# A fused forward and backward block on one core: a modulation row's ring moved behind the last fold, a fold through its other work tile, and bias rows in four row tiles

## The chip, the core and the metric

The kernel runs on one core of a Trainium2 chip. The metric is device time in microseconds of one execution. A core has a matrix engine (PE, with its weight loads PEld), a vector engine (DVE), a scalar engine (ACT), a general engine (POOL) and a sync engine (SP). Each executes its own instructions strictly in its own order; SP and POOL also issue the DMA transfers, so a transfer that waits on such a queue holds up all that stand behind it.

## The reference

One adaLN-conditioned block, forward and backward, batch 1, 2048 tokens, width 1024, hidden width 3584, all inputs in bf16:

```
mod = silu(c) @ w_mod                    # six rows of 1024: sa, ca, ga, sb, cb, gb
h = layernorm(x)*(1+ca) + sa
x = x + ga * irfft2(rfft2(h) * (w_r + 1j*w_i))
h = layernorm(x)*(1+cb) + sb
x = x + gb * (gelu(layernorm(h) @ w1 + b1) @ w2 + b2)
```

The outputs are x and the gradients, for a given grad_out, of x, w_r, w_i, w1, b1, w2, b2, c and w_mod. The gradient of w_mod is, for each of the six rows, an outer product of silu(c) with the gradient of that row, and the gradient of c needs the product of w_mod with it.

## The kernel before

The tokens are treated in four blocks of 512 (`NB = 4`), the hidden width in 28 chunks of 128, in groups of four (seven groups). A tile framework orders each engine's instructions from the order of the Python code and from priorities; `ordered()` (L670) pins PE's order by hand. It adds the waits: an instruction waits for the last writer of what it reads and for the last reader of what it overwrites. Tiles with the same `tag` share memory: a new one waits until the old one is no longer used.

The stages that matter here, in the order of time:

- **Forward MLP, about 388 to 768 us.** A written plan interleaves `z_block` (L782, the first product and the gelu) with `bo_pass` (L829, the second product). A `bo_pass` handles one block and one half (512 columns) of the width: four PSUM tiles `pbs`, one for each 128 tokens. Each is opened by a product of a row of ones with the bias row `b2_row` (L834, contraction length 1), and then accumulates 28 products (L843). ACT empties `pbs` (L852). At the end of a pass, `pa` (L862) sums over tokens, in four column tiles of 32. There are eight passes, so 32 bias products.
- **Backward through w1, block 0, about 768 to 820 us.** `pg_pass` (L934) multiplies the stored hidden gradient `gzr` (loaded from `d_gz`, L917) by w1, in two halves. ACT empties the result into `gn3` with row sums (L948). In the midst of it, `gmod5` (L994) reduces the gradient of modulation row 5 from `gacc`, stores it to `d_gmod` (L179), and runs `gmod_ring` (L968) for this row.
- **`gmod_ring`.** It loads the row into all partitions (`gr`, L976), and for each of eight 128-row parts of w_mod: loads the part (L973) into one of three buffers, reduces it against the row on DVE (L984), overwrites the buffer with the row times silu(c) (L986), and stores it to the output (L987, POOL). A buffer is loaded anew when its store has landed. In `gmod5` the buffers are `gmw` and `gmg`, in tags "ph" and "sb".
- **Backward blocks, about 820 to 1054 us** (the loop at L1080). For each block: loads of `n3u`, `n2u`, `got` (the output gradient), `pg_pass` for blocks 1 to 3; then on DVE and ACT the layer-norm gradient `ln_bwd` (L1026: a reduction L1028, two small steps L1030 and L1031, ACT L1032, and L1033); column sums over tokens on PE in strips of 32 columns (`sums3`, L196, into `acc3a`; `sums3_ga` into `acc3b`); a second layer-norm gradient (L1121); the add of the residual; the store of the sum to `d_gx1` (L1125, POOL); and then the fold: `g2` times the row `ga`, `fold_tok`, and `fold_d` into `fbuf2[:, b]`. All elementwise operations of two tensors go through `tt` (L172), so the profile shows them as L173. The fold works on two tiles, `g2` and `ftmp`; in block 3 `ftmp` is the tile of `gzr0`, which then becomes `ws2`.
- **Backward spectral part, from about 1054 us.** `s_fwd` (L466) multiplies `fbuf2` with a cosine or sine matrix (`pu`, L471, two PSUM tiles), emptied into `U` (L642); then eight `pair` steps with loads of `ws2` (L489 on SP, L490 on POOL), `pf` (L492) and so on. Between its steps PE is filled with products for the gradients of w2 (`gw2_product`, L1074) and w1. Each w2 chunk `fc` is emptied by ACT into `gwo[fc % 2]` (L1070) and stored by POOL (L1072). Their inputs come by transposing loads on SP (`hht`, `hhsA`, `otl` from `d_hh`, L1203; the first two into `fbuf2`, L1048). `gmod_ring` for rows 3 and 4 (`rows34`) runs beside the pairs, with buffers `gmy` and `sacc` in the tile `otl`, which has the memory of `got`.

## Time and profile before

| | us |
|---|---|
| three runs | 1496.75 (median), 1495.99, 1502.4 |
| the profiled execution | 1498.73 |
| its span, first to last instruction | 1496.9 |
| PE busy | 1407.9 (94%), 6703 instructions |
| DVE busy | 1069.7 (71%) |
| ACT busy | 721.7 (48%) |
| POOL busy | 359.1 (24%) |
| DMA | 324.27 MB, mean 217 GB/s |
| mean granted PE clock | 0.978 |

A "wait" is idle time of an engine ahead of an instruction, with what ended it. Products are pipelined: one of 128x512 is shown with 0.38 us, and at full clock they start 0.216 us apart.

### The profile page before, as it was taken

To read this page: it belongs to the slowest core of one execution; us is meant where nothing else is said; L and a number is where in the kernel's file an instruction comes from. 1 tells how busy PE (TensorE), PEld (TensorE's weight loads), DVE (VectorE), ACT (ScalarE), POOL (GpSimd) and SP (SyncE) were. 2 spreads that over 40 slices of the span, in tenths; PEclk is the share of its full clock that TensorE was granted. 3 is DMA by queue.
4 is the path that set the end of the run, shared out by engine and by line. 5 is a ranking of instruction groups with operands and counts; after the bars stand their busy time and mean duration, and the time that the engine had idled before them with its cause. 6 is when DMAs were issued, how large, how long until landed. Compare 5 with 4: busy or idle time off the path is not lost. (4 is left out here: it accounts for less than half of the span.)

```text
span 1496.9 us, 18191 instructions
## 1 busy us (share of the span) xinstructions
PE 1407.9 (94%) x6703; PEld 655.5 (44%) x6835; DVE 1069.7 (71%) x1574; ACT 721.7 (48%) x960; POOL 359.1 (24%) x421
## 2 busy tenths in 40 slices
PE   5899989999899999999999599999999999899998
PEld 2434545444344444444344244444444444444443
DVE  5883777898799888877411888987177676898533
ACT  4765546757787756666202133333622444453211
POOL 5710541211113122212111010021134421222323
PEclk8999999999999999999999799999999999999999
DMA  9962563899776777786997464396389977775995
GB/s 337 280 213 62 156 219 127 268 241 345 233 249 213 242 241 237 236 270 199 278 278 224 162 239 155 127 267 155 99 195 243 250 228 216 172 195 159 271 207 180
DMA packets 358040, 324.27 MB, mean 217 GB/s; under 512 B 209063, under 2 KB 300733, under 8 KB 357696
## 3 DMA queue, kind: packets, MB, share of 16 engines
q1 hardware_dynamic: 324160, 207.71, 51.8%
q0 software_dynamic: 33792, 115.40, 22.2%
q8 instruction: 53, 0.87, 0.2%
q14 instruction: 35, 0.29, 0.1%
HBM read 162.05 MB, written 111.20 MB: 183 GB/s over the span
## 5 line engine op out<-in xcount | busy, mean ns | idle before, releaser
L679 PE MATMUL pp<-gBoT,wt 128*128 128x512 bf16 x878 | 197.0, 381 | 5.1 <-DMA wt<-in_B_w_dram 2.1
L940 PE MATMUL pg<-w1T,gzr 128*128 128x512 bf16 x876 | 199.1, 386 | 1.3 <-issue 0.4
L1241 PE MATMUL gw1acc<-gzh,n3n 128*128 128x512 bf16 x876 | 194.5, 380 | 1.2 <-issue 0.2
L940 PEld LDWEIGHTS <-gzr 128*128 128x128 bf16 x896 | 88.0, 99 | 111.1 <-issue 10.8
L796 PEld LDWEIGHTS <-w 128*128 128x128 bf16 x896 | 87.7, 98 | 110.6 <-issue 7.2
L679 PEld LDWEIGHTS <-wt 128*128 128x128 bf16 x896 | 87.8, 98 | 109.3 <-issue 4.8
L1241 PEld LDWEIGHTS <-n3n 128*128 128x128 bf16 x896 | 87.7, 98 | 105.4 <-issue 1.8
L796 PE MATMUL pz<-n3Ta,w 128*128 128x512 bf16 x437 | 99.4, 383 | 4.4 <-ACT gt L799 3.5
L796 PE MATMUL pz<-n3Tb,w 128*128 128x512 bf16 x439 | 98.4, 379 | 0.5
L1065 PE MATMUL gw2acc<-gB,hhsA 128*128 128x512 bf16 x438 | 97.6, 379 | 0.7 <-issue 0.2
L843 PEld LDWEIGHTS <-hhA 128*128 128x128 bf16 x608 | 59.4, 99 | 74.4 <-issue 5.1
L799 ACT ACTIVATE gt<-pz,b_col 128x512 bf16<-128x512 f32 x112 | 73.1, 684 | 34.5 <-PE pz L796 31.4
L805 ACT ACTIVATE gt<-gt 128x2048 bf16<-128x2048 bf16 x28 | 53.5, 1910 | 67.0 <-DVE gt L173 67.0
L1245 ACT CAST gwo<-gw1acc 128x512 bf16<-128x512 f32 x53 | 30.7, 583 | 112.6 <-PE gw1acc L1241 87.4
L173 DVE TENSOR_TENSOR gt<-gt,gt 128x2048 bf16<-128x2048 bf16 x56 | 68.5, 1223 | 21.6 <-ACT gt L807 20.9
L173 DVE TENSOR_TENSOR ct<-ct 128x2048 bf16<-128x2048 bf16 x64 | 75.9, 1220 | 9.6 <-ACT ct L632 8.4
L1070 ACT CAST gwo<-gw2acc 128x512 bf16<-128x512 f32 x54 | 29.9, 584 | 99.6 <-PE gw2acc L1065 48.4
L1065 PEld LDWEIGHTS <-hhsA 128*128 128x128 bf16 x448 | 43.7, 98 | 52.1 <-DMA hhsA<-d_hh 0.6
L801 ACT ACTIVATE gt<-gt 128x2048 bf16<-128x2048 bf16 x28 | 53.4, 1908 | 0.6
L807 ACT ACTIVATE gt<-gt 128x2048 bf16<-128x2048 bf16 x28 | 53.4, 1907 | 0.5
L1246 POOL DMA_DIRECT2D out_dram<-gwo x56 | 30.7, 550 | 78.4 <-ACT gwo L1245 49.6
L1065 PE MATMUL gw2acc<-gB,otl 128*128 128x512 bf16 x187 | 44.0, 390 | 3.5 <-DMA otl<-d_hh 2.0
(318 smaller groups left out, 2496.0 us busy)
## 6 DMA issues: line engine op xcount, KB each, us to landing
gzr<-d_gz SPq DMA_DIRECT2D x28, 512.0 KB
wblk<-in_w_mod_dram SPq DMA_DIRECT2D x12, 1024.0 KB
d_ph<-pho POOLq DMA_DIRECT2D x21, 512.0 KB
out_dram<-otl POOLq DMA_DIRECT2D x40, 256.0 KB
d_hh<-hhA POOLq DMA_DIRECT2D x19, 512.0 KB
w2sD<-in_B_w_dram SPq DMA_DIRECT2D x14, 512.0 KB
hhC<-d_ph SPq DMA_DIRECT2D x14, 512.0 KB
w2sA<-d_ph SPq DMA_DIRECT2D x14, 512.0 KB
```

The lines of the kernel that those rows point to most:

```text
L173: return nc.vector.tensor_tensor(out=out, in0=a, in1=b, op=op)
L679: last_pe[0] = nc.tensor.matmul(pp[:], lhsT=wt[:, fg % 2, cch, k * P:(k + 1) * P], rhs=gBoT[j][:, cch, :], start=(cch == 0), stop=(cch == ...
L796: last_pe[0] = nc.tensor.matmul(pz[:], lhsT=w1s[g][:, cch, k * P:(k + 1) * P], rhs=n3T[:, cch, :], start=(cch == 0), stop=(cch == NDC - 1))
L799: nc.scalar.activation(out=zb[:, k, :], in_=pz[:], func=ACT.Identity, bias=b1_col[:, fc:fc + 1], scale=1.0)
L801: nc.scalar.activation(out=av, in_=zb, func=ACT.Square)
L805: nc.scalar.activation(out=sg, in_=bv, func=ACT.Sigmoid, scale=2.0 * GK)
L807: nc.scalar.activation(out=bv, in_=bv, func=ACT.Sigmoid, scale=-2.0 * GK)
L843: last_pe[0] = nc.tensor.matmul(pbs[i][:], lhsT=hh[:, k, i * P:(i + 1) * P], rhs=wp[:, k, :], start=False, stop=(g == 6 and k == 3))
L940: last_pg[0] = nc.tensor.matmul(pgs[i][:], lhsT=gzs[b, g][:, k, i * P:(i + 1) * P], rhs=w1Ts[g][:, k, h * KH:(h + 1) * KH], start=(g == 0 ...
L1065: nc.tensor.matmul(acc[:], lhsT=hh_of(fc)[:, t, :], rhs=gBs[t // 4][:, t % 4, h * KH:(h + 1) * KH], start=(t == 0), stop=(t == NT - 1))
L1241: nc.tensor.matmul(acc[:], lhsT=n3ns[t // 4][:, t % 4, cch * P:(cch + 1) * P], rhs=gz2[t // 8][:, t % 8, :], start=(t == 0), stop=(t == NT ...
L1245: nc.any.tensor_copy(out=ob, in_=acc[:])
```

## The change

Three edits:

1. The four token groups of a `bo_pass` get their bias from four copies of `b2_row`, in partitions 0, 32, 64 and 96, and each of the four products is placed in its own part of 32 rows of the array (`tile_position=(32 * i, 0)`). The row is loaded four times.
2. In the backward blocks, the first product of the fold (`g2` times `ga`) is written into `ftmp` instead of back into `g2`, and `fold_tok` and `fold_d` get the two tiles with their roles swapped.
3. `gmod_ring` for row 5 no longer runs in `gmod5`, but right ahead of where `rows34` is made, after the loop over the backward blocks, and with the buffers `gmy` and `sacc`. The reduction of the row and its store to `d_gmod` stay where they were.

```
-    b2_row = small.tile([1, D], BF16, name="b2_row", tag="gmrow", bufs=1)
+    b2_row = small.tile([P, D], BF16, name="b2_row", tag="gmrow", bufs=1)
     def after_ph():
-        nc.sync.dma_start(out=b2_row[:], in_=B_b2.rearrange("(o n) -> o n", o=1))
+        for i in range(4):
+            nc.sync.dma_start(out=b2_row[32 * i:32 * i + 1, :], in_=B_b2.rearrange("(o n) -> o n", o=1))
...
         for i in range(4):
             with ordered():
-                last_pe[0] = nc.tensor.matmul(pbs[i][:], lhsT=ones_bf[0:1, :], rhs=b2_row[0:1, cs_], start=True, stop=False)
+                last_pe[0] = nc.tensor.matmul(pbs[i][:], lhsT=ones_bf[32 * i:32 * i + 1, :],
+                                              rhs=b2_row[32 * i:32 * i + 1, cs_], start=True, stop=False,
+                                              tile_position=(32 * i, 0))
...
         store_gmod(g5, 5)
-        gmw = reg.tile([P, 2, D], BF16, name="gmw", tag="ph")
-        gmg = reg.tile([P, 2, D], BF16, name="gmg", tag="sb")
-        for _ in gmod_ring((5,), [gmw[:, 0], gmw[:, 1], gmg[:, 0]], gmg[:, 1, :]):
-            pass
...
         tt(au[:], g2[:], au[:], ALU.mult)
-        tt(g2[:], g2[:], bcn(ga_row, 4), ALU.mult)
-        fold_tok(g2, ftmp)
-        fold2_in[b] = fold_d(fbuf2[:, b], g2[:], ftmp)
+        tt(ftmp, g2[:], bcn(ga_row, 4), ALU.mult)
+        fold_tok(ftmp, g2[:])
+        fold2_in[b] = fold_d(fbuf2[:, b], ftmp, g2[:])
...
+    for _ in gmod_ring((5,), gmy, sacc):
+        pass
     rows34 = gmod_ring((3, 4), gmy, sacc)
```

In the built program the orders of PE and of ACT are the same as before, instruction for instruction. On DVE the ring's first reduction now stands after `fold_tok`'s first two steps of the last block, its first scaling after the next two, its second reduction after `fold_d`'s first two, and the other six steps behind the last fold; also the product into `gB3` stands two steps later in block 2's fold. On SP the ten loads of the ring left the stretch behind L1084 and L1086; the first transposing load into `fbuf2` comes ahead of `got`'s, the `gzr` loads of block 1 follow each other, and the first `pf` load is early, where a load of `gmg` was. The ring's loads now stand behind the four stores of `d_gmod` rows (L207): the row, one transposing load of `hht`, three w_mod loads, then one among the loads of `ws2`, and four ahead of those of `smi` and `hhsA`. On POOL the order behind the last store to `d_gx1` was three stores of `gwo` (chunks 3, 4, 5), four `ws2` loads, two stores of `gwo` (6, 7); it is now two stores of `gwo`, the ring's first store, four `ws2` loads, a store of `gwo`, three of the ring, one of `gwo`, three of the ring, one of `gwo`, one of the ring.

## The prediction

> **What bounds the kernel now.** I read the busy row first: PE works 1407.9 of 1496.9 us, so nearly every us that PE waits is a us of the span. PE's waits of over 0.3 us are 73 us together. The chain of waits (start, length, what) shows the largest of them:

> ```profile
> 801.76 7.33 SPq L1048
> 809.19 3.96 DMA gmg<-d_gmod
> 813.27 1.23 DVE gmw L984
> ```

> A transpose on SP's queue, then the load of the modulation row, then the ring of row 5 on DVE. PE's timeline (start, length, instructions, in brackets the idle time before) shows what hangs on it:

> ```profile
> 819.56 3.84 PE L940 MATMUL pg<-w1T,gzr 128*128 128x512 bf16 x17
> 839.97 0.61 PE L196 MATMUL acc3a<-gn3a,ones_bf 128*32 128x512 bf16 x2 [16.57 <-DVE gn3a L1033]
> ...
> 894.46 0.39 PE L196 MATMUL acc3a<-gn3b,ones_bf 128*32 128x512 bf16 x2 [2.65 <-DVE gn3b L1033]
> ...
> 948.70 0.39 PE L196 MATMUL acc3a<-gn3a,ones_bf 128*32 128x512 bf16 x2 [1.98 <-DVE gn3a L1033]
> ```

> In each backward block PE's first strip sum waits for DVE's first layer-norm gradient (L1033): 16.57, 2.65 and 1.98 us. DVE's timeline says why:

> ```profile
> 784.87 0.68 DVE L178 CAST row<-pq 1x512 bf16<-1x512 f32 x1 [0.18 <-PE pq L999]
> 813.27 1.23 DVE L984 CUSTOM_DVE_ANT_0 gmw<-gmw,gmg 128x1024 bf16<-128x1024 bf16 x1 [27.72 <-DMA gmg<-d_gmod]
> ...
> 834.15 1.22 DVE L1028 CUSTOM_DVE_ANT_0 got<-gn3a,n3u 128x1024 bf16<-128x1024 bf16 x1
> ...
> 877.02 2.29 DVE L173 TENSOR_TENSOR gn3a<-gn3a,rows 128x4096 bf16<-128x4096 bf16 x1 [3.02 <-DMA d_gx<-gn3a]
> ```

> DVE stands 27.72 us at the head of the ring, runs it to 834.15, and only then starts block 0, though ACT had emptied the products by 820.2. The last row is the fold's first product, in place, waiting for the store of the same tile. A wait also costs clock (window, length, busy times and counts, granted clock, DMA):

> ```profile
> 840.00:844.00 4.00, 3.78 (x10) 1.36 (x11) 3.77 (x8) 0.43 (x1) 0.00 (x0) 0.50 0.50 178
> 844.00:848.00 4.00, 4.00 (x20) 1.82 (x19) 3.13 (x3) 1.94 (x2) 0.00 (x0) 1.00 0.12 41
> ```

> After the 16.57 us, products run at half the granted clock, 0.43 us apart, then at full clock 0.216 us apart. The same happens after 2.65 us (0.53 at 895 to 898) and 1.98 us (0.50 at 950 to 953).

> **Row 5's ring leaves block 0.** PE and ACT have the same instructions in the same order in both programs. DVE loses at this place eight pairs of 1.22 + 0.48 us and all waits on them. The layer-norm gradient then needs the last evacuation, 820.2; from the first L1030 to the strip sum took 837.06 to 839.97, 2.9 us; so the strip can start near 823.6, and PE is there at 819.56 + 3.84 = 823.4. The wait falls from 16.57 to 0.2: **-16.4**. From this strip to the next ones PE took 839.97 to 851.17, 11.2 us, for 42 products; at full clock 42 x 0.216 + 0.6 = 9.7: **-1.5**. The next strips need pru, 9.7 us after the first strip (849.65): just in time. Loads: SP's queue loses ten ring loads, some of which waited for stores. The first hh transpose moves ahead of got's load into a gap where SP waited (782.4 to 796.5); the gzr loads of block 1 no longer stand between ring loads and come when PE frees the slots, to 819. The bounds are 0 (something else as late as the ring) and 18.1 us.

> **The fold's first product into the other tile.** It no longer waits for the store; the next step does, since it writes the stored tile. Of the 3.02 us (2.78 in block 1) the 2.29 us of the product are hidden. DVE ends each block 2.3 us earlier and PE, without the slow clock, 1.5 us earlier. In block 1 DVE's two L1028 (2.4 us) and the small steps then still end after PE's evacuation, so a wait of about 1.0 of 2.65 stays; in block 2 about 0.3 of 1.98. Waits of 0.82 and 1.27 us later in the trace (1182, 1216) are followed by full clock, so the slow 1.5 us go too: **-3.1 and -3.2**. Bounds: 0, if DVE stays as far behind, and -7.6, both waits and both slow stretches gone. In block 3 PE waits for nothing here.

> [...]

> **The ring behind the last fold.** Two of its reductions and one scaling now stand inside the last fold on DVE: 2 x 1.22 + 0.48 = 2.9 us, against 2.3 hidden there. From the end of the residual add (1032.8) to fbuf2 complete (1054.1) it was 21.3 us; now 21.9. By then PE is 24.2 us earlier than before and DVE 26.0 (22.7 at the start of block 2, 1.0 in its waits for PE's strips and evacuations, 2.3 in its fold), so pu isn't late by that. The ring's first loads go out when got is free (the same 1032.8), the w_mod ones behind one hht transpose (3.6 to 6 us on SP, rows 1032.84 and 1036.54); they land some 10 us after, and the reduction stands at 11.8 because the 1 MB store took 9.1. So they are just covered; each us later is a us on fbuf2, beyond 1 us of slack. What follows on SP (smi, two hhsA) has some 14 us of slack before PE needs it. The rest of the ring, six steps, lies where DVE was idle for 15.3 and 15.7 us (1054 to 1085).

> The new wait is on POOL. ACT and POOL, before:

> ```profile
> 1044.45 0.54 POOL L1072 DMA_DIRECT2D out_dram<-gwo  x1 [9.38 <-ACT gwo L1070]
> 1054.35 1.02 POOL L490 DMA_INDIRECT ws<-in_A_w_r_dram,xu  x1 [9.36 <-DVE fbuf L173]
> ...
> 1050.90 0.59 ACT L1070 CAST gwo<-gw2acc 128x512 bf16<-128x512 f32 x1 [2.86 <-PE gw2acc L1065]
> 1054.37 0.59 ACT L1070 CAST gwo<-gw2acc 128x512 bf16<-128x512 f32 x1 [2.88 <-PE gw2acc L1065]
> 1055.18 0.59 ACT L642 CAST U<-pu 128x512 bf16<-128x512 f32 x1 [0.22 <-PE pu L471]
> ```

> The store of gw2's chunk 5 (1044.45) left ahead of the four ws loads. In the new order it stands behind the ring's first store and those four. Counted from the residual add: scaling done at 15.9, gzr0 free and ws loads from 18.3, four times 1.3, the store at 23.5, landed at 26 to 28. ACT's two gwo casts of chunk 7 write the same slot and wait for it, and the U casts stand right behind them, due at 24.0. pu has two buffers, so PE waits about 3.5 us at its third column block, plus 1.5 of slow clock: **+5.0**, between 0 (store of gx1 lands in 6 us, as in other blocks) and +10.

> **b2's rows in four tiles.** Three more 2 KB loads near 111 us, where SP then idles to 126: nothing. On PE (first two rows the bias, last two a column-tiled sum):

> ```profile
> 743.03 1.03 PE L834 MATMUL pbo<-b_row,ones_bf 1*128 1x512 bf16 x4
> 743.99 3.63 PE L843 MATMUL pbo<-w2sC,hhA 128*128 128x512 bf16 x16
> ...
> 751.00 0.40 PE L862 MATMUL pa<-otile,ones_bf 128*32 128x512 bf16 x4
> 751.33 3.63 PE L843 MATMUL pbo<-w2sB,hhB 128*128 128x512 bf16 x16
> ```

> The bias occupies 0.96 us, the four column tiles 0.33. Row tiles don't occur in the trace; four products in four parts of the array are nearest to the latter, so 0.63 per group. Of eight groups six count (460, 520, 567, 620, 667, 743 us), since 388 is ahead of a wait for ACT (3.54 us at 407) and 713 holds one (1.86 us): **-3.8**. Bounds: -5.0, all eight; +2.3, if each of the four positions costs the 0.095 us that entering and leaving cost now, and nothing overlaps.

> [...] The trace shows 0.31 instead of 0.216 us on both sides of the present group already, so nothing is added.

> **Sum.** -16.4 - 1.5 - 3.1 - 3.2 + 5.0 - 3.8 = -23.0 us on the profiled execution of 1498.73: 1475.7. The median of the runs is 2.0 us lower: **1474**.

> **Rivals.**
> - The tiles don't overlap: PE's -3.8 falls away, 1478. For it: no row tile in the trace. Against: the column tiles.
> - POOL's order costs nothing: without +5.0, 1469. For it: other gx1 stores landed in 5.8 to 7.0 us, which brings all of that chain forward by 2 to 3 us. Against: the 9.1 us came with hht transposes on the same DMA engines, and these stay.
> - DVE is the bound of blocks 1 and 2, and the fold's 2.3 us go to something else that is late (au, a gzr tile): without -6.3, 1480. For it: DVE is busy 8 to 9 tenths of these slices. Against: the store is its longest wait in each fold, and the other inputs landed before they were needed.
> - Slower: the ring's loads come late at the last fold. DVE runs in order, so fbuf2, the ws loads, the chunk 5 store and PE's pu all wait. With X us of lateness the time is 1474 + X - 1: slower than before from X = 24, by over 0.5% from 31. For it: DVE stood 27.72 us for such a row, and 24.1 us for another in the tail (gr). Against: that was SP's order; from its issue the row landed in 4 us. With X = 33, 1506.

> **Chances.** Forecast 0.54 (own range 1470 to 1478, with tile and store bounds), tiles 0.10, no POOL wait 0.12, DVE-bound 0.16, ring late 0.08. About 0.5% (7.5 us) is what a measurement of this kernel can tell from no change. The first four lie below 1489; I move 0.04 of the DVE case, whose lateness may be larger, to no change, with 0.03 of the ring's: faster 0.88, same 0.07, slower 0.05. The range, 1466 to 1486, takes in the ends of the bias tiles and of the POOL wait and the DVE case.

> **What would show it.** The first strip sum near 820 us (3.8 earlier by the tiles) with under 0.5 us before it; granted clock 1.00 from there; the next two with 1 us or less; no DMA row ahead of the fold's first product, a short one ahead of its second step; at pu an idle of 3 to 4 us with ACT waiting for out_dram<-gwo; L834's four starting within 0.02 us. Wrong would be a new wait of several us in block 0 or 1, or DVE idle for otl inside the last fold.

## The result, and the profile after

The changed kernel takes 1483.89 us (median of 6 runs, 1479.81 to 1487.43) against 1497.95 us of the kernel before in the same comparison: ratio 0.9906, 95% interval 0.9879 to 0.9934, so 14 us faster, where the forecast had 23. 1483.89 lies inside the forecast's range of 1466 to 1486 us, but not inside 1470 to 1478, the range of the main case alone. The profiled execution is the slowest of the six: 1487.43 us, span 1485.5.

PE's timeline of the changed kernel, at the strips that were shown of before (start, length, instructions, idle before):

```profile
821.86 0.39 PE L196 MATMUL acc3a<-gn3a,ones_bf 128*32 128x512 bf16 x2
...
831.59 0.39 PE L196 MATMUL acc3a<-pru,ones_bf 128*32 128x512 bf16 x2 [0.38 <-DVE pru L173]
...
873.76 0.39 PE L196 MATMUL acc3a<-gn3b,ones_bf 128*32 128x512 bf16 x2 [1.52 <-DVE gn3b L1032]
...
925.23 0.39 PE L196 MATMUL acc3a<-gn3a,ones_bf 128*32 128x512 bf16 x2 [0.27 <-DVE gn3a L1032]
```

The 16.57 us are gone, 2.65 became 1.52, 1.98 became 0.27. DVE's timeline shows the reasons: it now waits until ACT begins to deliver the second half of block 0 (32.09 us) instead of for a ring, and the wait for the store has moved from the fold's first product to its second step and shrunk.

```profile
783.26 0.68 DVE L178 CAST row<-pq 1x512 bf16<-1x512 f32 x1 [0.18 <-PE pq L1002]
816.03 1.23 DVE L1027 CUSTOM_DVE_ANT_0 got<-gn3a,n3u 128x1024 bf16<-128x1024 bf16 x1 [32.09 <-ACT gn3a L951]
...
858.64 2.36 DVE L173 TENSOR_TENSOR gn3a<-pru 128x2048 bf16<-128x2048 bf16 x2 [1.24 <-DMA d_gx<-gn3a]
```

The loss stands at the start of the spectral part. PE, ACT, POOL and DVE there:

```profile
1029.60 2.06 PE L471 MATMUL pu<-smA,fbuf 128*128 128x512 bf16 x8
1039.34 0.59 PE L471 MATMUL pu<-smA,fbuf 128*128 128x512 bf16 x1 [7.69 <-ACT U L642]
...
1022.94 0.59 ACT L1069 CAST gwo<-gw2acc 128x512 bf16<-128x512 f32 x1 [2.25 <-PE gw2acc L1064]
1037.73 1.07 ACT L1069 CAST gwo<-gw2acc 128x512 bf16<-128x512 f32 x2 [14.20 <-DMA out_dram<-gwo]
1038.69 1.09 ACT L642 CAST U<-pu 128x512 bf16<-128x512 f32 x2
...
1026.09 0.54 POOL L990 DMA_DIRECT2D out_dram<-otl  x1 [15.54 <-DVE otl L989]
1028.34 1.75 POOL L490 DMA_INDIRECT ws<-in_A_w_r_dram,xu  x1 [1.71 <-DVE gn3a L173]
...
1034.15 0.97 POOL L490 DMA_INDIRECT ws<-in_A_w_i_dram,xu  x1 [0.30 <-issue]
1035.12 0.58 POOL L1071 DMA_DIRECT2D out_dram<-gwo  x1
...
1021.89 1.23 DVE L987 CUSTOM_DVE_ANT_0 otl<-otl 128x1024 bf16<-128x1024 bf16 x1 [4.46 <-DMA otl<-in_w_mod_dram]
```

Read from the bottom: DVE waits inside the last fold for the ring's first w_mod tile; the ring's first store leaves at 1026.09, the four `ws` loads follow, and only then, at 1035.12, the store of gw2's chunk 5. ACT's casts of chunk 7 wait 14.20 us for it, the U casts stand behind them, and PE, which could go on at 1031.66, goes on at 1039.34. The granted clock behind it (window, length, busy times and counts of PE, PEld, DVE, ACT and POOL, clock, DMA share, GB/s):

```profile
822.00:826.00 4.00, 3.95 (x19) 1.78 (x19) 3.66 (x8) 0.55 (x1) 0.00 (x0) 1.00 0.00 0
...
1039.00:1043.00 4.00, 3.44 (x8) 1.31 (x9) 1.13 (x1) 1.42 (x4) 0.00 (x0) 0.50 0.89 297
```

Block 0 runs at full clock; pu's eleven products after the wait run at half.

Where the time went, as the shift of the same product between the two profiled executions (after minus before):

| point | shift, us | of this stage |
|---|---|---|
| first bias group (388) | -0.2 | |
| first `pg` (768) | -1.6 | -1.4 |
| second strip of block 0 (851) | -19.6 | -18.0 |
| second strip of block 2 (960) | -24.9 | -5.3 |
| `acc3b` of block 3 (997) | -24.5 | +0.4 |
| second half of `pu` (1068) | -14.0 | +10.5 |
| last product (1490) | -11.5 | +2.5 |

### The profile page after: what moved, and what is told of

Its sections match the earlier page's. It is cut to its first block, busy times and chain, and to the rows that moved or that the text cites. A ratio compares the mean times of both kernels' runs of the same rounds, so it can differ in the third digit from the quotient of the medians.

```text
span 1485.5 us, 18204 instructions
## 1 busy us (share of the span) xinstructions
PE 1402.2 (94%) x6703; PEld 653.7 (44%) x6835; DVE 1069.0 (72%) x1574; ACT 720.3 (48%) x960; POOL 362.6 (24%) x421
## 4 chain that ended last, share of the span: by engine, by line
PE 32%; DVE 31%; issue 16%; DMA 9%; ACT 8%; POOL 4%; SPq 0%; POOLq 0%; DVEq 0%; ACTq 0%
PE pbo L846 9%; PE pz L797 5%; DVE ct L173 5%; DVE gt L173 4%; PE pu L471 4%; PE pg L943 3%; PE gw2acc L1064 3%; PE pv L564 3%; DVE got L1027 2%; DMA out_dram<-otl 2%; PE gw1acc L1240 1%; ACT ct L461 1%; PE pp L679 1%; DVE st L437 1%; DVE w2sA L817 1%
## 5 line engine op out<-in xcount | busy, mean ns | idle before, releaser
L943 PE MATMUL pg<-w1T,gzr 128*128 128x512 bf16 x876 | 194.6, 379 | 1.6 <-ACT gn3b L951 0.2
L173 DVE TENSOR_TENSOR gt<-gt,gt 128x2048 bf16<-128x2048 bf16 x56 | 68.5, 1223 | 21.6 <-ACT gt L808 20.9
L173 DVE TENSOR_TENSOR ct<-ct 128x2048 bf16<-128x2048 bf16 x64 | 75.8, 1219 | 10.7 <-ACT ct L632 8.8
L987 DVE CUSTOM_DVE_ANT_0 otl<-otl 128x1024 bf16<-128x1024 bf16 x24 | 29.0, 1223 | 51.7 <-DMA otl<-in_w_mod_dram 45.3
```

The costliest lines, as they stand in the source:

```text
L173: return nc.vector.tensor_tensor(out=out, in0=a, in1=b, op=op)
L943: last_pg[0] = nc.tensor.matmul(pgs[i][:], lhsT=gzs[b, g][:, k, i * P:(i + 1) * P], rhs=w1Ts[g][:, k, h * KH:(h + 1) * KH], start=(g == 0 ...
```

## The experiments

Every kernel was timed in five rounds against the kernel before on the same chip. Three edits alone first, and the pair of the last two.

**The bias alone** (edit 1; the rest as before).

> Only the b2 rows in four tiles; fold and ring as before. Theory (the tiles overlap, but what they save is taken back by waits for ACT and DVE at 407, 534 and 713 us): 0.5 to 1.5 us faster than before, about 1497; L834's four products of a group within 0.02 us of each other, the gaps at 407 and 713 longer than before by about as much as the group became shorter. Rival, the forecast's term: 3.8 us faster, about 1494, with those gaps unchanged. Rival, no overlap: no gain, the four products 0.2 us apart.

1493.70 us against 1496.44, ratio 0.9985 (0.9972 to 0.9999). The products overlap. In the changed kernel, bias group and neighbour:

```profile
742.05 0.39 PE L835 MATMUL pbo<-b_row,ones_bf 1*128 1x512 bf16 x4
742.38 3.63 PE L846 MATMUL pbo<-w2sC,hhA 128*128 128x512 bf16 x16
```

Four products start within 0.02 us and the next one 0.33 us later, where it was 0.96. The median lies between the first theory and the forecast, and the interval (0.1 to 4.2 us gained) cuts off none but zero. Of the three waits that the first theory named, the one at 407 us grew from 3.54 to 4.31 us, the one at 534 us (0.50) is new, and the one at 713 us grew from 1.86 to 2.08. The profile tells more and is taken up below.

**The fold alone** (edit 2).

> Only the fold's first product into the other work tile; ring in block 0 and bias as before. Theory (the fold is what is late in blocks 1 and 2, and each wait of about 2 us brings half clock behind it): the 16.57 us of block 0 stay, the waits of 2.65 and 1.98 us fall below 1.6 and 0.5, no half clock behind them, 6 us faster, about 1492. Rival, the waits alone count and the clock does not: 3.3 us faster, about 1494.5. Rival, DVE is late there for another reason: no change.

1494.62 us, ratio 0.9991 (0.9978 to 1.0004): 1.3 us, not resolved from zero. Yet the profile shows that the theory's part happened: from 851 to 1018 us the strips moved from -0.7 to -6.9, 6.2 us. At `pu` 4.5 us of it are given back (the shift is -2.4 at 1083 us), which no theory had said:

```profile
1051.72 10.48 PE L471 MATMUL pu<-smA,fbuf 128*128 128x512 bf16 x39 [2.66 <-ACT U L642]
...
1041.80 1.87 POOL L490 DMA_INDIRECT ws<-in_A_w_r_dram,xu  x1 [13.68 <-DVE gn3a L173]
...
1046.53 0.95 POOL L490 DMA_INDIRECT ws<-in_A_w_i_dram,xu  x1 [0.31 <-issue]
1047.49 1.16 POOL L1072 DMA_DIRECT2D out_dram<-gwo  x2
```

There is no ring here, and still the chunk 5 store stands behind the `ws` loads. In the kernel before it left ahead of them, at 1044.45, and the loads waited for `fbuf`. With the tiles swapped, `ws2`'s memory is last read one step earlier (released by `gn3a`, not `fbuf`). So the order on POOL came with the fold edit, where the prediction had put it down to the ring; that the earlier release is the reason is likely, but no run separates it. The two profiled executions lie 5.8 us apart (1498.73 and 1492.89), the medians 1.8: what the edit is worth alone is taken from the ratio, and only the places from the profile.

**The ring alone** (edit 3).

> Only the ring of row 5 moved behind the last fold; fold in place and bias as before. Theory (block 0 gives 18 us, and the pu stage takes 10 back, since the store of gw2's chunk 5 stands on POOL behind the ring's first store and four ws loads): the 16.57 us fall below 0.5, waits of 2 to 3 us stay in blocks 1 and 2, a wait of about 8 us at pu, about 8 us faster, 1490. Forecast's terms: 17.9 less and 5.0 more, 13 us faster, 1485. Rival, the ring's loads are late for the last fold: the wait stands at the first pu product (fbuf), not at the ninth.

1485.95 us, ratio 0.9934 (0.991 to 0.9958): 10 us. Block 0 gives 18.0 us and the waits of blocks 1 and 2 stay (3.37 and 1.92), as expected, but the wait at `pu` is another:

```profile
1039.76 2.61 PE L471 MATMUL pu<-smA,fbuf 128*128 128x512 bf16 x6 [3.19 <-DVE fbuf L173]
...
1033.31 0.54 POOL L1068 DMA_DIRECT2D out_dram<-gwo  x1
...
1041.11 1.75 POOL L490 DMA_INDIRECT ws<-in_A_w_r_dram,xu  x1 [1.71 <-DVE fbuf L173]
```

Here the store is ahead of the `ws` loads, and PE waits for the fold itself, which in place begins behind the store of gx1 and then waits 4.91 us for the w_mod tile. For this kernel the rival was right: the ring's loads are late for the last fold.

**Fold and ring, no tiles.**

> The changed kernel with the bias rows as before. Theory (the tiles bring about 1 us in this kernel too): 1484 to 1486, and the stages up to the first weight-gradient pass (pg) are 1 to 1.5 us longer than in the changed kernel. Rival, the forecast's 3.8 us: 1487.5. The pu wait is 7 to 8 us in both.

1485.17 us, ratio 0.9917 (0.9894 to 0.9939), with 6.53 us at `pu` for U. Block 2 ends 5 us earlier than with the ring alone, but the ninth product of `pu` starts at 1039.34 in both this and the changed kernel, and the ring alone went on at 1039.76: what PE gains in blocks 1 and 2 it waits for at `pu`.

**The store of chunk 5 on another queue.** One line of the changed kernel:

```
-            nc.gpsimd.dma_start(out=out_6[...], in_=gwo[:, fc % 2])
+            (nc.scalar if fc == 5 else nc.gpsimd).dma_start(out=out_6[...], in_=gwo[:, fc % 2])
```

> The changed kernel with one edit: the store of gw2's chunk 5 is issued from ACT's queue, right behind the casts that fill its slot, and so no longer stands on POOL behind the ring's first store and the four ws loads. Theory (that store's place on POOL makes the whole pu wait): the casts of chunk 7 start as soon as their products are done, the wait of 7.7 us at pu's ninth product falls below 1 and the eleven products at half clock behind it go: 9 to 10 us faster than the changed kernel, about 1474. Rival (the last fold is late, because DVE waits 4.5 us for the ring's first w_mod tile): the wait stays at 6 us or more and only changes its name to fbuf; 1483. Half way: if both count, a wait of 2 to 4 us.

1473.76 us against 1496.05, ratio 0.9843 (0.9816 to 0.987); the changed kernel had 0.9906. PE and ACT:

```profile
1029.28 14.29 PE L471 MATMUL pu<-smA,fbuf 128*128 128x512 bf16 x62
...
1020.48 0.37 ACTq L1071 DMA_DIRECT2D out_dram<-gwo  x1
...
1029.48 0.59 ACT L1069 CAST gwo<-gw2acc 128x512 bf16<-128x512 f32 x1 [2.87 <-PE gw2acc L1064]
1030.66 0.59 ACT L642 CAST U<-pu 128x512 bf16<-128x512 f32 x1 [0.59 <-PE pu L471]
```

The 62 products run without a gap. DVE still waits 4.65 us for the w_mod tile, and `fbuf` is still late by it: that alone costs PE nothing here. The theory holds, and the rival, by which the wait would only have changed its name, falls: with this one store off POOL's queue the stage gives back 0.3 us (shift -24.8 to -24.5) instead of 10.5.

**The ring behind the whole fold.**

```
-    for _ in gmod_ring((5,), gmy, sacc):
-        pass
+    with tc.issue_after(fold2_in[3].ins):
+        for _ in gmod_ring((5,), gmy, sacc):
+            pass
```

> The changed kernel, with the ring held back until the last step of the last fold (fbuf) has been issued; the chunk 5 store stays on POOL behind the ws loads. Theory: DVE's 4.5 us wait for a w_mod tile and 2.9 us of ring steps leave the fold, fbuf is complete 7 us earlier, the ws loads start 6 us earlier and the store behind them too; the pu wait falls to 1 to 2 us: 7 to 8 us faster than the changed kernel, about 1476. Rival (the wait comes from the number of transfers ahead of the store, not from the time at which they start): the wait falls by less than 3 us, 1481 or more.

1476.48 us, ratio 0.9866 (0.9842 to 0.9891). POOL and PE:

```profile
1023.89 1.87 POOL L490 DMA_INDIRECT ws<-in_A_w_r_dram,xu  x1 [12.00 <-DVE gn3a L173]
...
1031.05 0.58 POOL L1071 DMA_DIRECT2D out_dram<-gwo  x1
...
1035.28 12.85 PE L471 MATMUL pu<-smA,fbuf 128*128 128x512 bf16 x50 [2.46 <-ACT U L642]
```

Counted from the end of the residual add, the loads start at 14.8 instead of 20.7 us and the store at 21.9 instead of 27.5. The wait falls from 7.69 to 2.46 us, with eight products at half clock behind it. So both things feed the wait: when the fold finishes (5.2 of its 7.69 us) and how much stands ahead of the store. Moving the store is enough to end it, but the ring's place inside the fold is a cause of it too.

**Both.**

> Both edits. Theory: no wait at pu, 9 to 10 us faster than the changed kernel, 1474, no more than the store from ACT's queue alone, since one of the two is enough. Rival (each removes its own part of the wait): 2 us or more faster than either alone.

1472.31 us, ratio 0.9845 (0.9818 to 0.9871): no wait at `pu`, and the same as with the store alone (0.9843). This kernel and the one with the store alone are the fastest of the study, some 9 us faster than the changed one by their ratios (0.0061 and 0.0063 of 1498 us).

**The ring beside the inverse transform.** No ring behind the fold; row 5 is the first of the rows that run beside the products:

```
-    for _ in gmod_ring((5,), gmy, sacc):
-        pass
-    rows34 = gmod_ring((3, 4), gmy, sacc)
+    rows34 = gmod_ring((5, 3, 4), gmy, sacc)
...
-            if 3 - k < (1, 2, 2, 2, 2, 2, 3, 3)[n]:
+            if 3 - k < (1, 3, 3, 3, 3, 4, 4, 4)[n]:
```

> The changed kernel with the ring of row 5 run as the first eight of the 24 steps that stand beside the inverse transform's products, and no longer behind the last fold. Theory: nothing of it touches the last fold or pu; the wait at pu is 1 to 2 us (the chunk 5 store still stands behind the ws loads), 7 us faster than the changed kernel, 1477, if the 13.6 us of DVE steps fit beside the transform, where PE waits for DVE nowhere now. Rival (they do not fit: the hh transposes on SP come behind more loads that wait for stores, and PE waits for them): new waits of 2 us and more for hhsA or R between 1060 and 1240, 1485 or more.

1498.80 us, ratio 1.0014 (0.9995 to 1.0033). At `pu` 2.52 us are left, where the theory had 1 to 2, but then the rival's waits come:

```profile
1140.60 8.54 PE L1064 MATMUL gw2acc<-gB,hhsA 128*128 128x512 bf16 x31 [7.59 <-DMA hhsA<-d_hh]
...
1161.51 10.01 PE L1064 MATMUL gw2acc<-gB,otl 128*128 128x512 bf16 x32 [3.73 <-DMA otl<-d_hh]
...
1214.45 5.69 PE L1064 MATMUL gw2acc<-gB,otl 128*128 128x512 bf16 x16 [5.12 <-ACT gwo L1069]
```

PE's shift against before goes from -20.4 (1113) to -8.5 (1180) and to -0.4 (1241). The first 12 us are the hh transposes: SP's queue carries the ring's loads ahead of them. The other 8 us are two waits for `gwo` casts (1.31 us at 1206 and the 5.12 us above) with half clock behind the longer one (16 products in 5.69 us); ACT, which makes these casts, stands 19.13 us there for `xt` (12.72 in the changed kernel), whose load leaves POOL's queue right behind a store of the ring. So the stretch behind the last fold is a better place for the ring than this one.

**Controls for the store.** The same line of the store, in the kernels with one or two edits.

> The kernel before with the fold edit and the chunk 5 store on ACT's queue; ring in block 0. Theory (the fold edit alone already puts the ws loads ahead of that store on POOL, which is where 4 of its 6 us went): the 2.66 us wait at pu and the half clock behind it go, 6 us faster than before, about 1490. Rival (the fold's gain was lost elsewhere): no faster than with the fold edit alone, 1494 to 1495.

1495.64 us against 1499.68, ratio 0.9972 (0.9952 to 0.9992). The wait at `pu` is gone and PE is 7.2 us earlier at 1113 us; then waits of 1.26, 1.80 and 1.77 us for hh transposes and 3.36 us for V take it to 3.2 (1200) and 2.7 (1283). The step of the theory is right; its end is between theory and rival, since more is late behind it.

> The kernel before with the ring edit and the chunk 5 store on ACT's queue; fold in place. Theory (here PE waits for fbuf itself, whose fold starts late behind the store of gx1 and DVE's wait for a w_mod tile): the 3.19 us wait for fbuf stays, no faster than with the ring edit alone, 1486. Rival (the store is what counts here too): 4 us faster, 1482.

1490.93 us, ratio 0.9951 (0.9937 to 0.9965), against 0.9934 without the line: not faster. The wait for `fbuf` stays, 3.18 us, as the theory has it.

> The best-so-far version (the changed kernel with the chunk 5 store on ACT's queue) without the bias tiles. Theory: with no wait at pu to take it back, what is left of the tiles is five groups of 0.64 us less the longer waits at 407 and 534 us, 1.5 to 2.5 us: 1475 to 1476.5. Rival, the forecast's 3.8 us: 1477.5. Rival, nothing: 1474.

1480.07 us against 1499.68, ratio 0.9863 (0.9842 to 0.9883), with 0.9843 for the same kernel with tiles, on another chip. The difference, 0.0020 of 1498 us, is 3 us, with both intervals wider than that. On the scale of that chip the ratio gives 1475.6 us (0.9863 of 1496.05), which fits the theory and does not exclude its rivals.

## Why the prediction was right or wrong

- **Ring out of block 0** (-16.4 - 1.5 = -17.9): -18.0 measured. The strip starts at 821.86, the next one 9.7 us later (9.7 forecast), and the wait is gone. (820.2 + 2.9 makes 823.1, where the forecast wrote 823.6; 0.4 us pass between the last evacuation and that small step, and 821.86 is 823.5 without the 1.6 us by which PE came early from the stage ahead.) The "ring late" rival was a live one: the sign that the forecast named for it, DVE idle for `otl` inside the last fold, came (4.46 us). With the fold in place PE waited 3.19 us for it; in the changed kernel it reached PE through POOL's queue (below). Both are far from the 24 us at which this rival would have made the kernel slower than before.
- **Blocks 1 and 2** (-6.3): -5.3 in the changed kernel (1.52 us left of the first wait, 0.27 of the second, forecast 1.0 and 0.3), -6.2 with the fold alone. The mechanism is right and the DVE rival wrong. What the forecast missed is that PE, coming earlier to `pu`, waits there for `U`: alone, the edit brings 1.3 us, and 4.2 us with the chunk 5 store moved (ratio 0.9972).
- **POOL's order at `pu`** (+5.0, bounds 0 to +10): +10.5, past the upper bound. This is the term that failed, by its size; the chain was the forecast one, link by link. From the end of the residual add, the ring's scaling was done at 18.1 us (forecast 15.9), because the w_mod load landed 14.2 us after the add and not some 10: SP issued it at 6.1 us, behind the hht transpose, and it took 8.1 us, where the forecast had seen the load of the modulation row land in 4. The store of gx1 took 7.1 us and not 9.1, so DVE came 2 us earlier than forecast, too; the forecast said "just covered", and DVE stood 4.46 us. The `ws` loads began at 20.7 (18.3) and took 6.8 us (5.2), the store was issued at 27.5 (23.5), U came at 31.0, when PE needed it at 24.0. Wait 7.69 (3.5), half clock for eleven products, about 2.4 us (1.5). The load added 2.2 us, the `ws` loads 1.6 and the half clock 0.9, all in the same direction, and lateness that is handed on through queues adds up. Which edit set the order was wrong too: it was the fold, probably by freeing `ws2`'s memory a step earlier.
- **Bias tiles** (-3.8): -1.4 in the changed kernel up to the first `pg`. Each of five groups gave 0.63 to 0.65 us (60.21 to 59.57 us from one group to the next, 53.31 to 52.67, 46.40 to 45.76), as forecast; the overlap rival is wrong. What took it back lay at two places that were counted at 0 or as a gain. At 534 us PE came early enough to wait for DVE's `w2sD` (L868): 1.33 us in the changed kernel, 0.5 to 2.6 us in the six kernels with tiles, nothing over 0.3 in the seven without. At 713 the wait for ACT's `otile` grew from 1.86 to 2.07 us, and the half clock behind it: 29.6 to 31.1 us for this group, against 27.95 to 27.97 in five of the seven kernels without tiles and 29.65 in the other two. Behind this wait two stretches of 3.41 us ran at half clock in four of the kernels with tiles and one in the other two; without tiles it was one in two kernels and none in five, so a part of the loss came in some profiles and not in others (last section). From the first bias group to the first `pg`, six profiles with tiles average 378.5 us, seven without 378.8. The comparisons of runs give 2.2 us for the tiles alone, with an interval that barely leaves out zero, and 1.6 and 3.0 us across chips, within their intervals. What the tiles bring as a whole, between nothing and about 3 us, stays open.
- **Behind `pu`** (0 forecast): +2.5. A wait for an hh transpose of 2.09 us at 1142 us is new, with seven products at half clock; as a wait of 1.99 us for another transpose at 1171 us, in the kernel before, is gone, this leaves 1.0 us by 1180 us. Another 1.3 us are lost near 1350 us, where a wait for `ct` (1.95 us) was followed by half clock and the one of before (2.34 us) was not. The kernel with the fold and no `pu` wait showed the same: PE comes earlier, SP's transposes don't.
- **The clock behind waits of 2 us** (3.0 of the 6.3 us): with the fold alone the strips gained 6.2 us, more than the two waits together (2.65 + 1.98 = 4.63), so their half clock did cost time. But the forecast's reading, that such a wait always brings half clock, is not borne out: behind a wait of 2.14 us at 1170.72 in the changed kernel the granted clock stayed 1.00 (last section).

Between the two profiled executions there are 11.3 us (1498.73 - 1487.43), where the terms sum to 23.0. Of the 11.7 that are missing, 5.5 are the `pu` term, 2.4 the bias, 2.5 what is lost behind `pu`, and 1.0 blocks 1 and 2; the rest is 0.4 us and less at each place. By the medians 9 us are missing and not 11.7, since the second profiled execution lies 3.5 us above its median.

## What to carry to other kernels

When an edit moves PE forward by 20 us, follow each transfer that used to be early behind that place: when it is issued can be the next bound, as here. A store from a double buffer is such a transfer: what was queued ahead of it on POOL's queue here was time of the engine that refills the buffer (ACT's 14.20 us); where the refilling engine has a queue of its own, issue it there (some 9 us for one line here, but nothing where PE waited for the fold itself). And where several links of a chain each have an unknown, add their upper ends for the range: here three of them were late together.

## What the runs showed of the hardware

All that follows is read or counted in the profiles of this study's thirteen kernels, from the idle times of PE and the record of the granted clock. Whether a wait of PE was followed by half clock was not a matter of its length alone. In the thirteen profiles there are 91 waits of over 0.7 us between 380 and 1245 us. Behind the 26 of up to 1.82 us no product ran at half clock. Behind the 15 of 3.88 us and more, always (7 to 13 products). Of the 50 from 1.85 to 3.80 us, 31 were followed by half clock, and 19 were not, for the same instruction too: the wait for `otile` of 1.85 to 1.86 us in two of seven kernels, the first strip of block 1 after 2.65 us in the kernel before and not after 2.48 us with the bias alone:

```profile
890.00:894.00 4.00, 3.32 (x16) 1.50 (x17) 4.00 (x7) 0.39 (x1) 0.00 (x0) 1.00 0.26 101
894.00:898.00 4.00, 4.00 (x20) 1.83 (x19) 2.91 (x7) 2.38 (x2) 0.00 (x0) 1.00 0.12 14
```

In the changed kernel, 2.09 us ahead of the product at 1142.50 were followed by a clock of 0.50 (1143.49 to 1146.90), and 2.14 us ahead of the one at 1170.72 by 1.00.

```profile
946.40:949.81 3.41, 1.43 (x8) 0.59 (x7) 2.45 (x3) 2.06 (x2) 0.00 (x0) 1.00 0.58 208
949.81:953.22 3.41, 3.41 (x10) 1.21 (x8) 2.69 (x8) 0.93 (x1) 0.00 (x0) 0.50 0.00 0
```

PE was busy for 1.43 us of the first cell, so it was idle for 1.98, and the next cell ran at half clock. In the changed kernel the cell from 1030.86 had 2.62 us of idle PE and half clock behind it, the one from 1167.40 had 2.14 us and full clock behind it. Of all cells at full clock between 380 and 1245 us, the 31 with 2.3 us of idle PE or more were all followed by half clock, and none of the 3157 with less than 1.48 us; of the 28 between, 15 were. (Ends of products are modelled and some records are missing, which may blur this border.) The waits for `otile` of 1.85 to 1.86 us put 1.37 and 1.54 us into one cell in the two kernels in which they cost clock (the 1.54 us in the kernel before, where PE's idle time in that cell was 1.65 us in all), and 0.96 to 1.24 us in the other five. So in these profiles half clock went with the idle time within one cell more closely than with the length of the whole wait; no run was made to test that this is the cause. As an estimate from these counts, a wait of 1.85 to 3.8 us costs its length, and in about 6 cases of 10 some 1.7 us more (one cell, 8 products at 0.43 instead of 0.216 us); in 5 of the 31 such waits that were followed by half clock two cells ran so, 15 or 16 products.
